# Sliding-window attention into an ELU layer pair on one core: two pairs taken together, casts and value copies moved to other engines, one batch's loads moved

## The chip, the cores and the metric

The kernel runs on one core of one Trainium2 chip. The metric is the device time of one execution in microseconds, lower is better. A core has a matmul engine (PE), a vector engine (DVE), an engine for activation functions (ACT), a general engine (POOL) and a synchronizing engine (SP). Each works through its own queue in order. SP, ACT and POOL also issue DMA transfers from their queues.

## The reference, cut to what matters

```python
# q, k, v: (8 batches, 8 heads, 576 positions, 64), float32
scores = (1 / sqrt(64)) * q @ k.transpose(0, 1, 3, 2)
scores = where(abs(pos[:, None] - pos[None, :]) <= 32, scores, -1e9)
attn = exp(scores - max(scores)); attn = attn / (sum(attn) + 1e-9)
x = (attn @ v) -> (4608 tokens, 512)          # heads side by side
h = x @ w_in                                  # w_in (512, 2048)
g = where(h > 0, h, exp(min(h, 0)) - 1)
out = g @ w_out                               # w_out (2048, 512), float32
```

## The kernel before, in words

Attention and the two dense layers run interleaved, in an order that is written out by hand (`tc.manual_schedule()`, L59): each engine's queue holds its instructions in the order in which the program emits them.

**The dense layers.** 4608 tokens make 18 tiles of 256. Of the 16 blocks of 128 hidden columns a step takes two, so a tile has 8 steps and the whole 144; the last loop (L639 ff.) counts them as `kk`. The first 16 steps alternate between tiles 0 and 1, from step 16 on tile t holds steps 8t to 8t+7. In step kk, `elu(kk-1)` emits one DVE instruction, g_sb (L607); then the tasks of slot "dve"; then `mm1(kk)` emits 8 matmuls 128x256 on PE (L583), the exponential e_sb on ACT (L590) and m_sb = e_sb - 1 on DVE (L596); then slot "mid"; then `mm2(kk-2)` emits 4 matmuls 128x512 (L622) and, at a tile's last step, one copy of y on ACT and one on DVE with their two output transfers on SP (L634, L635); then slot "end". `mm1` has two buffers, h0 and h1, in turn, so `mm1(kk+2)` needs g_sb of step kk to have been read out, and `mm2` needs g_sb as its weights.

**Attention.** Queries are taken in blocks of 64; a pair (`i`, 36 of them, two for each tile of the dense layers) is two blocks of all 8 heads. Against 128 keys per block: `scores` (32 products in pairs of heads, L297), `exponential` (ACT, 128x1024, L308), `mask` (DVE, L317), `pv` (L329, values with a column of ones), `normalize` (DVE, reciprocal and product, L338 and L341). The result x_st then goes to xT, the dense layers' operand, either by PE (`x_transpose`, L350, and `x_evac` on ACT) for pairs up to 9, or by a DMA transpose on SP (`x_dma`, L367) from pair 10 on. The scores, the products and the x transpose of a pair use one PSUM buffer of two banks, "s" or "u". `begin` (L509) gives each pair's first step. Pairs before 8 go one at a time, from `FIRST_TWO` on two together: scores in one step in "s" and "u", exponentials in that step and the next, masks one step later each, both products two steps after the scores, normalizing three and four steps after. Buffer "u" shares its banks with tile 1's y sums, and is theirs until step 18 (`swap_back`).

**What attention needs.** A batch has 4.5 pairs; batch 2 is first used by pair 9, batch 3 by pair 13, batch 4 by pair 18. Queries and keys are loaded as float32 by SP (`load_qk`, two transfers each, L123), cast to bf16 (`cast_qk`, on ACT or DVE by L227 and L229) and transposed. For batch 2 PE does that in four groups of nine with an evacuation by ACT (`transpose_qk`, L272, into qT and kT). From batch 3 on the cast rows are written to DRAM by a transfer from ACT's queue (`write_rows`, L253) and read back by a DMA transpose on SP (`transpose_rows`, L258). The casts of a batch from 3 on, six of them, go to the ends of the first free steps from `c0` on: steps in which no pair's scores or second exponential stand.

**Values.** `load_v` (POOL, L142, casting on the way) writes five blocks of 128 positions that start at -32: V_e, three buffers in turn. Odd query blocks need blocks shifted by 64, V_o: `rotate_v` (DVE, L153) copies halves of 64 partitions across, 64x1040 elements each, four instructions a batch. `hold_v` (L147) zeroes one row again on DVE: a load that follows has to wait for it.

Of the kernel before, what the change touches and what calls it, by code (L numbers as in the profile page):

```python
# [21 lines left out]
def kernel(  # L22
# [9 lines left out]
    nc = tc.nc  # L32
# [14 lines left out]
    VS = 5  # L47
# [46 lines left out]
    def ps_tile(shape, dt, tag, name):  # L94
# [7 lines left out]
          for i in range(2)]  # L102
    V_e = [cpool.tile([128, VS, H, VD], BF16, name=f"Ve{i}") for i in range(3)]
    V_o = [cpool.tile([128, VS - 1, H, VD], BF16, name=f"Vo{i}")
           for i in range(3)]
# [6 lines left out]
    WHOLE, HALF_A, HALF_B = (0, SJ), (0, SJ // 2), (1, SJ // 2)  # L112
# [37 lines left out]
    def rotate_v(b, m0, m1, parts=(0, 1)):  # L150
        e, o = V_e[b % 3], V_o[b % 3]
        for z in parts:
            nc.vector.tensor_copy(o[64 * z:64 * (z + 1), m0:m1],  # L153
                                  e[64 * (1 - z):64 * (2 - z),
                                    m0 + z:m1 + z])

# [30 lines left out]
    def edges(i):  # L189
# [19 lines left out]
        out=masks, in_=masks, compare_op=ALU.is_ge, fill=0.0,  # L209
        base=0, pattern=[[0, 5], [-1, QB]], channel_multiplier=1)  # L210
    nc.gpsimd.affine_select(
        out=masks, in_=masks, compare_op=ALU.is_ge, fill=0.0,
# [157 lines left out]
    def first_pair(b):  # L370
        return NQB * b // 2
# [27 lines left out]
    for mi in (0, 4):  # L399
        nc.gpsimd.affine_select(  # L400
            out=masks[:, mi, :], in_=masks[:, mi, :], compare_op=ALU.is_ge,
            fill=0.0, base=-WIN, pattern=[[0, QB]], channel_multiplier=1)
    nc.gpsimd.affine_select(
        out=masks[:, 3, :], in_=masks[:, 3, :], compare_op=ALU.is_ge,
# [16 lines left out]
    for i, tag in ((0, "s"), (1, "u")):  # L421
        scores(i, tag)
        exponential(i)
    idle(4, "y0")
    rotate_v(0, 0, 2)
    for i in (0, 1):
        mask(i)
# [34 lines left out]
    def at(kk, slot, fn, *args):  # L462
        tasks.setdefault((kk, slot), []).append((fn, args))
# [18 lines left out]
    for i in (2, 3):  # L482
        at(0, "mid", rotate_v, 0, 2, VS - 1, (i - 2,))
        at(0, "mid", mask, i)
        at(1, "mid", pv, i)
        at(2, "dve", normalize, i)
        at(3, "mid", x_transpose, i)
        at(3, "mid", x_evac, i, nc.scalar)
# [11 lines left out]
    for m in range(VS):  # L500
        at(16 + m, "mid", load_v, 2, m)
    at(12, "dve", rotate_v, 1, 0, 2)
    for z in range(2):
        at(14 + z, "dve", rotate_v, 1, 2, VS - 1, (z,))

    FIRST_TWO, FIRST_DMA, BACK_AT = 8, 10, 18
    begin = {4: 9, 5: 12, 6: 17, 7: 19, 8: 25, 10: 30, 12: 37}  # L509
    for i in range(FIRST_TWO, NPAIR):  # L510
        begin[i] = begin.get(i - i % 2, STEPS * (i // 2) - 14)
    for i in range(4, NPAIR):
        two = i >= FIRST_TWO
        kk, z = begin[i], i % 2 if two else 0
        at(kk, "end" if i == 4 else "mid", scores, i,
           "u" if z or i == 7 else "s")
        at(kk + z, "end" if i == 4 else "mid", exponential, i)
        at(kk + 1 + z, "dve", mask, i)
        at(kk + (2 if two else 1), "end", pv, i)
        n = kk + (3 + z if two else 2)  # L520
        at(n, "dve", normalize, i)
        if i < FIRST_DMA:
            at(n, "end", x_transpose, i)
            at(n, "end", x_evac, i, nc.scalar)
        else:
            at(n, "end", x_dma, i)
# [3 lines left out]
    for b in range(2, B):  # L530
        k0 = begin[first_pair(b)]

        l_qk, l_v, c0 = {2: (0, 0, 0), 3: (15, 24, 22)}.get(
            b, (k0 - 28, k0 - 22, k0 - 22))
        if b >= 3:
            at(l_qk, "mid", load_qk, b, 0, WHOLE)
            at(l_qk + 1, "mid", load_qk, b, 1, WHOLE)
            for m in range(VS):
                at(l_v + m, "mid", load_v, b, m)
        for n, back in enumerate((3, 2, 1, 0) if b == 2 else (10, 8, 3, 2)):  # L540
            m0 = 2 * (n // 2)
            at(k0 - back, "dve", rotate_v, b, m0, m0 + 2, (n % 2,))
        if b == 2:

            for n, (which, j0) in enumerate(((0, 0), (0, 9), (1, 0), (1, 9))):
                at(19 + n, "mid", cast_qk, b, which, WHOLE, j0, 9, nc.vector)
                at(20 + n, "mid", transpose_qk, b, which, WHOLE, j0, 9,
                   nc.scalar, "s")
            continue


        free = [f for f in range(c0, k0) if f not in starts]
        for n, (which, j0) in enumerate(
                (which, j0) for which in range(2) for j0 in (0, 6, 12)):
            at(free[n], "end", cast_qk, b, which, WHOLE, j0, 6,
               nc.vector if free[n] < 24 else nc.scalar)
            if j0 == 12:
                at(free[n], "end", write_rows, b, which)
                at(free[n] + (3 if free[n] == 29 else 4), "mid",
                   transpose_rows, b, which)  # L560
# [121 lines left out]
```

## Time and profile before

| what | us |
|---|---|
| median of 3 runs | 309.61 (308.73 to 309.79) |
| the profiled execution | 307.99 |
| its span, first to last instruction | 306.3 |
| PE busy | 295.2 |
| DVE busy | 245.5 |
| ACT busy | 169.1 |
| POOL busy | 47.9 |

The profile is one execution. Its times count from the span's first instruction. A timeline row gives start, length, engine, line, operation, what is written and read, how many were merged (x8), and in brackets idle time of the engine before it with what ended it. In the rows of a queue (SPq, ACTq) the length is that of issuing, waits within the issue included. "Start to start" is the distance between the starts of two neighbours on an engine: neighbouring instructions of ACT and DVE overlap by about 0.1 us, so their lengths can't be summed. The steps' places in the trace are told by the L583 groups: one opens at the start of each step (step 6 at 28.06, step 18 at 54.67, step 37 at 97.16).

### The profile page before, as it was taken

The page shows a single profiled execution, that of the slowest core. Times are in us where ns is not written, and L with a number is a line of the kernel's source. Part 1 is how long each engine was busy: PE and PEld are TensorE (multiplying, and loading weights), DVE is VectorE, ACT ScalarE, POOL GpSimd, SP SyncE. Part 2 cuts the span into 40 slices and gives each one's busy share as a digit, 9 for nine tenths or more (in the row PEclk, how much of TensorE's full clock was granted, in tenths as well). Part 3 has the DMA queues.
Part 4 walks back from the last instruction along what each step waited for, and adds up shares of the span by engine and source line. Part 5 has one row for each costly group of instructions (what it writes and reads, how often), then busy time and mean ns, then how long its engine had stood idle before and what let it go on. Part 6 is the DMA issues. An engine that isn't in the chain of part 4 may idle for free.

```text
span 306.3 us, 7611 instructions
## 1 busy us (share of the span) xinstructions
PE 295.2 (96%) x3083; PEld 196.6 (64%) x3083; DVE 245.5 (80%) x476; ACT 169.1 (55%) x254; POOL 47.9 (16%) x68
## 2 busy tenths in 40 slices
PE   7779999999999999999999999999999999999994
PEld 2466666676665666666666666666666666666662
DVE  6777688999978887988798879887988787877663
ACT  3663647677654674676367636763535353533431
POOL 8836002860220311111111100000000000000000
PEclk9999999999999999999999999999999999999999
DMA  9999999999999499999999897396111111111011
GB/s 188 186 205 205 183 295 411 280 148 176 270 250 190 40 253 257 294 220 218 161 321 195 226 227 276 111 196 144 68 36 71 34 71 35 71 36 68 0 70 68
DMA packets 91653, 51.74 MB, mean 169 GB/s; under 512 B 76515, under 2 KB 81635, under 8 KB 91619
## 3 DMA queue, kind: packets, MB, share of 16 engines
q0 software_dynamic: 42880, 10.10, 42.9%
q1 hardware_dynamic: 46866, 34.42, 41.8%
q10 hardware_dynamic: 1872, 6.75, 6.6%
q8 instruction: 24, 0.39, 0.6%
q14 instruction: 11, 0.08, 0.1%
HBM read 36.70 MB, written 15.34 MB: 170 GB/s over the span
## 4 chain that ended last, share of the span: by engine, by line
PE 84%; DVE 9%; ACT 2%; DMA 2%; issue 2%; ACTq 0%; DVEq 0%
PE ps L583 38%; PE psY L622 37%; PE psS L297 3%; PE psS L329 3%; DVE g_sb L607 2%; DMA f<-in_k_dram 2%; DVE pm L317 2%; DVE x_st L341 1%; DVE Vo L153 1%; DVE m_sb L596 1%; ACT pu L308 1%; PE psXT L350 1%; PE ptx L272 1%; ACT e_sb L590 1%; DVE y_sb L229 1%
## 5 line engine op out<-in xcount | busy, mean ns | idle before, releaser
L590 ACT ACTIVATE e_sb<-ps 128x512 f32<-128x512 f32 (+1 forms) x145 | 86.2, 595 | 121.8 <-PE ps L583 116.4
L583 PE MATMUL ps<-xT,w_in_sb 128*128 128x256 bf16 x1152 | 149.2, 273 | 1.0 <-DVE g_sb L607 0.6
L622 PE MATMUL psY<-w_out_sb,g_sb 128*128 128x512 bf16 x576 | 147.4, 379 | 0.0
L583 PEld LDWEIGHTS <-w_in_sb 128*128 128x128 bf16 x1152 | 110.8, 98 | 39.5 <-issue 1.6
L607 DVE SCALAR_TENSOR_TENSOR g_sb<-ps,m_sb 128x512 bf16<-128x512 f32 (+1 forms) x145 | 99.4, 686 | 12.5
L596 DVE TENSOR_SCALAR m_sb<-e_sb 128x512 bf16<-128x512 f32 x144 | 61.9, 430 | 35.6 <-ACT e_sb L590 33.6
L622 PEld LDWEIGHTS <-g_sb 128*128 128x128 bf16 x576 | 54.5, 98 | 38.6 <-DVE g_sb L607 0.2
L142 POOL DMA_DIRECT2D Ve<-in_v_dram x40 | 35.2, 888 | 123.4 <-PE psS L329 96.3
L308 ACT ACTIVATE pu<-psS 128x1024 bf16<-128x1024 f32 x36 | 36.5, 1019 | 1.6 <-PE psS L297 1.6
L341 DVE TENSOR_TENSOR x_st<-psS,rc 128x512 bf16<-128x512 f32 x36 | 24.9, 691 | 1.2
L317 DVE TENSOR_TENSOR pm<-pu,masks 128x1024 bf16<-128x1024 bf16 x36 | 24.6, 682 | 1.2 <-ACT pu L308 1.2
L227 ACT CAST qkb<-f 128x768 bf16<-128x768 f32 (+1 forms) x29 | 24.3, 838 | 0.0
L329 PEld LDWEIGHTS <-pm 128*64 128x64 bf16 x576 | 11.2, 110 | 11.3 <-DVE pm L317 8.2
L329 PE MATMUL psS<-Ve,pm 128*64 128x65 bf16 x320 | 13.9, 196 | 1.9 <-DVE pm L317 1.8
L153 DVE COPY Vo<-Ve 64x1040 bf16<-64x1040 bf16 x32 | 14.1, 442 | 1.2 <-DMA Ve<-in_v_dram 0.2
L229 DVE COPY y_sb<-psY 128x512 f32<-128x512 f32 x18 | 12.3, 685 | 1.0 <-PE psY L622 0.9
L329 PE MATMUL psS<-Vo,pm 128*64 128x65 bf16 x256 | 12.5, 197 | 0.5 <-DVE pm L317 0.2
L297 PEld LDWEIGHTS <-kT 64*128 64x128 bf16 x576 | 9.5, 95 | 5.1 <-issue 4.2
L297 PE MATMUL psS<-qT,kT 64*128 64x64 bf16 x576 | 11.9, 191 | 0.5 <-DVE kT L229 0.5
L227 ACT COPY y_sb<-psY 128x512 f32<-128x512 f32 x18 | 10.5, 582 | 2.2 <-PE psY L622 2.2
L227 ACT COPY qT<-ptx 128x1152 bf16<-128x1152 bf16 (+2 forms) x8 | 7.5, 971 | 3.2 <-PE ptx L272 2.4
L229 DVE CAST qkb<-f 128x1152 bf16<-128x1152 f32 (+3 forms) x11 | 7.7, 724 | 1.0 <-DMA f<-in_k_dram 0.6
(36 smaller groups left out, 70.9 us busy)
## 6 DMA issues: line engine op xcount, KB each, us to landing
out_dram<-y_sb SPq DMA_DIRECT2D x35, 256.0 KB, 2.5
f<-in_q_dram SPq DMA_DIRECT2D x12, 576.0 KB, 6.8
f<-in_k_dram SPq DMA_DIRECT2D x12, 576.0 KB, 7.4
in_dram<-qkb ACTq DMA_DIRECT2D x10, 576.0 KB, 4.8
Ve<-in_v_dram POOLq DMA_DIRECT2D x24, 128.0 KB, 7.2
w_in_sb<-in_moe_w_in_dram POOLq DMA_DIRECT2D x4, 512.0 KB, 9.9
w_out_sb<-in_moe_w_out_dram POOLq DMA_DIRECT2D x4, 512.0 KB, 12.8
Ve<-in_v_dram POOLq DMA_DIRECT2D x16, 96.0 KB, 7.4
```

The lines of the kernel that those rows point to most:

```text
L142: nc.gpsimd.dma_start(out=V_e[b % 3][p0:p1, m, :, 0:D], in_=v[b, :, lo + p0:lo + p1, :].rearrange("h p d -> p h d"))
L227: nc.scalar.copy(d_, s_)
L297: nc.tensor.matmul(psS[:, h % 2, hp * 128 + z * QB:hp * 128 + (z + 1) * QB], lhsT=kT[b % 2][base:base + 64, KPAD + hp * S + QB * qb - WIN: ...
L308: nc.scalar.activation(pu, _bap(psS, [psS.ap[0], [1, 1024]]), AX.Exp, scale=SCALE)
L317: nc.vector.tensor_mul(pm, pu, _bap(mm, [mm.ap[0], [0, H], [1, 2 * QB]]))
L329: nc.tensor.matmul(psS[QB * z:QB * (z + 1), par, hp * VD:(hp + 1) * VD], lhsT=pm[:, par * HP + hp, z * QB:(z + 1) * QB], rhs=vv[:, qb // 2 ...
L341: nc.vector.tensor_mul(x_st, _bap(psS, [psS.ap[0], [VD, HP], [512, 2], [1, D]]), _bap(rc, [rc.ap[0], [2, HP], [1, 2], [0, D]]))
L583: nc.tensor.matmul(ps[:, j, :], lhsT=w_in_sb[:, do, fo * 128:(fo + 1) * 128], rhs=xT[t][:, :, do, :], start=(do == 0), stop=(do == NDO - 1))
L590: nc.scalar.activation(e_sb, ps, AX.Exp)
L596: nc.vector.tensor_scalar(m_sb, e_sb, -1.0, None, ALU.add)
L607: nc.vector.scalar_tensor_tensor(g_t[kk][:, z * w:(z + 1) * w, :], ps, 0.0, m_t[kk][z], ALU.max, ALU.min)
L622: nc.tensor.matmul(psY[t][ts], lhsT=g_sb[:, j, ts * 128:(ts + 1) * 128], rhs=w_out_sb[:, s * FG + j, :], start=(s == 0 and j == 0), stop=( ...
```

## The change

Five things change; all lie between steps 15 and 58.

- Pairs 6 and 7 are taken together: `FIRST_TWO` is 6. Both scores go to step 18 (before 17 and 19), both products to step 20 (18 and 20), normalizing and x transposes to steps 21 and 22 (19 and 21). Pairs 8 and 9 begin at 26 in place of 25, pairs 10 and 11 at 31 in place of 30.
- Batch 2's casts stand at steps 18, 20, 21 and 23 (before 19 to 22), and the second and third are on ACT (all were on DVE). Its four groups of transposes stand at steps 22 to 25 (before 20 to 23), in "s" and "u" in turn (all in "s" before).
- The shifted copies of batches 2 and 3 are made by two SP transfers each, at steps 21 and 28, in place of eight DVE copies. Those of later batches stay on DVE.
- Batch 3's casts: free steps are now 22 to 25, 28, 29 (before 22, 23, 24, 27, 28, 29), and four of the six are on DVE (before two).
- Batch 4's loads of queries and keys stand at the end of step 35 (before the middle of steps 30 and 31, and so in SP's queue between batch 3's transposes of queries and of keys). Its values' loads keep their place in the program from step 36 on, but a `hold_v` at step 36 now holds them; before, POOL issued them as its queue got there, the first at 78.34 us, in step 28. Its casts begin at step 41 (before 36). The values' loads of batches 5 to 7 get a `hold_v` each too, and loads of queries and keys go to the ends of their steps in place of the middles.

In SP's queue the order becomes: queries of batch 3, tile 0's y, keys of batch 3, tile 1's y, shifted copies of batch 2, tile 2's y, shifted copies of batch 3, transposes of batch 3's queries and keys, tile 3's y, x transposes of pairs 10 and 11, queries and keys of batch 4.

```diff
+    def rotate_v_dma(b):
+        e, o = V_e[b % 3], V_o[b % 3]
+        for z in range(2):
+            nc.sync.dma_start(out=o[64 * z:64 * (z + 1), 0:VS - 1],
+                              in_=e[64 * (1 - z):64 * (2 - z), z:z + VS - 1])
...
-    FIRST_TWO, FIRST_DMA, BACK_AT = 8, 10, 18
-    begin = {4: 9, 5: 12, 6: 17, 7: 19, 8: 25, 10: 30, 12: 37}
+    FIRST_TWO, FIRST_DMA, BACK_AT = 6, 10, 18
+    begin = {4: 9, 5: 12, 6: 18, 8: 26, 10: 31, 12: 37}
...
-           "u" if z or i == 7 else "s")
+           "u" if z else "s")
...
-        l_qk, l_v, c0 = {2: (0, 0, 0), 3: (15, 24, 22)}.get(
+        l_qk, l_v, c0 = {2: (0, 0, 0), 3: (15, 24, 22), 4: (35, 36, 41)}.get(
             b, (k0 - 28, k0 - 22, k0 - 22))
         if b >= 3:
-            at(l_qk, "mid", load_qk, b, 0, WHOLE)
-            at(l_qk + 1, "mid", load_qk, b, 1, WHOLE)
+            at(l_qk, "end", load_qk, b, 0, WHOLE)
+            at(l_qk + (b != 4), "end", load_qk, b, 1, WHOLE)
+            if b > 3:
+                at(l_v, "dve", hold_v, b)
             for m in range(VS):
                 at(l_v + m, "mid", load_v, b, m)
-        for n, back in enumerate((3, 2, 1, 0) if b == 2 else (10, 8, 3, 2)):
-            m0 = 2 * (n // 2)
-            at(k0 - back, "dve", rotate_v, b, m0, m0 + 2, (n % 2,))
+        if b <= 3:
+            at((21, 28)[b - 2], "mid", rotate_v_dma, b)
+        else:
+            for n, back in enumerate((10, 8, 3, 2)):
+                m0 = 2 * (n // 2)
+                at(k0 - back, "dve", rotate_v, b, m0, m0 + 2, (n % 2,))
         if b == 2:
             for n, (which, j0) in enumerate(((0, 0), (0, 9), (1, 0), (1, 9))):
-                at(19 + n, "mid", cast_qk, b, which, WHOLE, j0, 9, nc.vector)
-                at(20 + n, "mid", transpose_qk, b, which, WHOLE, j0, 9,
-                   nc.scalar, "s")
+                at((18, 20, 21, 23)[n], ("mid", "end", "end", "mid")[n],
+                   cast_qk, b, which, WHOLE, j0, 9,
+                   (nc.vector, nc.scalar, nc.scalar, nc.vector)[n])
+                at(22 + n, "mid", transpose_qk, b, which, WHOLE, j0, 9,
+                   nc.scalar, "su"[n % 2])
             continue
...
             at(free[n], "end", cast_qk, b, which, WHOLE, j0, 6,
-               nc.vector if free[n] < 24 else nc.scalar)
+               nc.vector if free[n] < 26 else nc.scalar)
```

## The prediction

> **What bounds the kernel now.** I read, in this order: the page, PE's timeline (start of every first-layer group, L583, which opens a step), what PE waited for, then the timelines of ACT, DVE and SP around each late step, and the DMA table. Step n is iteration kk = n of the last loop.
>
> ```profile
> span 306.3 us, 7611 instructions
> PE 295.2 (96%) x3083; PEld 196.6 (64%) x3083; DVE 245.5 (80%) x476; ACT 169.1 (55%) x254; POOL 47.9 (16%) x68
> ```
> PE sets the end. But its busy time is modelled, so I take the distance between starts of the L583 groups instead.
>
> ```profile
> 74.02 1.04 PE L583 MATMUL ps<-xT,w_in_sb 128*128 128x256 bf16 x8
> ...
> 75.76 1.04 PE L583 MATMUL ps<-xT,w_in_sb 128*128 128x256 bf16 x8
> ...
> 80.44 0.40 PE L350 MATMUL psXT<-ident,x_st 128*128 128x128 bf16 x4 [0.26 <-DVE x_st L341]
> 80.68 1.04 PE L583 MATMUL ps<-xT,w_in_sb 128*128 128x256 bf16 x8
> ...
> 95.43 1.03 PE L583 MATMUL ps<-xT,w_in_sb 128*128 128x256 bf16 x8 [0.56 <-DVE g_sb L607]
> ```
> Step 26 (74.02 to 75.76) is a bare step: 1.74. What attention adds, from undisturbed steps: scores of one pair 0.44 (52.49 to 54.67), of two 0.68 (97.16 to 99.58); values' product of one pair 0.47 (43.41 to 45.63), of two 0.73 (101.32 to 103.79); nine transposes 0.50; an x transpose 0.23. From step 38 (99.58) on every step has its sum. The starts of steps 17 to 37:
> ```
> 17 52.49  18 54.67  19 57.20  20 59.62  21 62.34  22 64.81  23 67.05
> 24 69.63  25 71.61  26 74.02  27 75.76  28 78.27  29 80.68  30 82.64
> 31 85.06  32 86.80  33 89.49  34 91.24  35 92.97  36 95.43  37 97.16
> ```
> Length less sum of contents (step 28, say: 2.40 - 1.74 - 0.23 = 0.43): late are step 18 by 0.32, 23 by 0.34, 24 by 0.24, 27 by 0.05, 28 by 0.43, 32 by 0.22, 35 by 0.72, together 2.32 us; PE waits for DVE each time the profile names one. That is all the change can win beside PE work itself. Steps 14 and 15 lose 0.4 more, untouched.
>
> ```profile
> 93.70 0.42 DVE L153 COPY Vo<-Ve 64x1040 bf16<-64x1040 bf16 x1
> 94.16 0.43 DVE L596 TENSOR_SCALAR m_sb<-e_sb 128x512 bf16<-128x512 f32 x1
> 94.69 0.69 DVE L607 SCALAR_TENSOR_TENSOR g_sb<-ps,m_sb 128x512 bf16<-128x512 f32 x1
> ```
> The late g_sb of step 35 stands behind a shifted copy of batch 3's values. One limit stands close behind:
>
> ```profile
> 77.96 1.22 SPq L123 DMA_DIRECT2D f<-in_q_dram  x2
> 79.22 2.19 SPq L123 DMA_DIRECT2D f<-in_k_dram  x2
> 90.56 5.02 SPq L258 DMA_TRANSPOSE kT<-in_dram  x1
> ```
> ```profile
> kT<-in_dram SPq DMA_TRANSPOSE x5, 7.8
> ```
> The first three are SP's issues (start, length), the last the median from issue to landing. Batch 3's keys land at 90.56 + 7.8 = 98.4; step 37 reads them at 98.13 + 0.34 = 98.47. Any gain ahead of step 37 would be lost to this landing if it stayed put. (Landings of single transfers below are the trace's semaphore records.)
>
> **The Trainium skill.** "SBUF — State Buffer", section "Who interferes with whom": copies and casts of DVE in two-port modes and a GpSimd instruction exclude each other. The trace agrees in kind: L153 takes 424 ns at least and 871 beside POOL's issues. "DMA: Bandwidth & Descriptors", section "Issuing engines are not separate DMA queues": transfers of all queues share 16 engines and interleave. The trace fits: batch 3's keys took 6.3 us into DRAM (84.19 to 90.54) beside batch 4's loads, 3.6 (72.05 to 75.62) without.
>
> **Part by part.**
> ```profile
> 63.42 0.60 ACT L590 ACTIVATE e_sb<-ps 128x512 f32<-128x512 f32 x1 [0.94 <-PE ps L583]
> 63.92 1.28 ACT L227 COPY qT<-ptx 128x1152 bf16<-128x1152 bf16 x1
> 65.09 0.58 ACT L227 COPY xT<-psXT 128x512 bf16<-128x512 bf16 x1
> ```
> ACT's prices are taken start to start like these, where it is never idle: e_sb 0.50, evacuation of nine transposes 1.17, x evacuation 0.49, cast 128x1152 1.04 (47.21 to 48.25), cast 128x768 0.73, y 0.49, own DMA issue 0.7. DVE: g 0.60, m 0.53, mask 0.60, reciprocal and x_st about 0.9, y 0.60, shifted copy 0.45.
>
> *Pairs 6 and 7 together.* Scores go from steps 17 and 19 to 18, products from 18 and 20 to 20. PE saves 2 x 0.44 - 0.68 = 0.20 and 2 x 0.47 - 0.73 = 0.21. Step 18's stall goes: mask 6 now has two steps. Next late: pair 7's scores need the two banks of tile 1's y; DVE's y copy ends about 1.15 after step 18 starts, the scores come at 1.30: free by 0.15, and a shortfall costs itself.
>
> *Casts and transposes of batch 2, one or two steps later.* Two 128x1152 casts leave DVE (2 x 0.67) for ACT (2 x 1.04); batch 3 gives DVE two 128x768 casts more (2 x 0.47) and takes them from ACT (2 x 0.73). DVE's late steps 23 and 24 (0.34 + 0.24) should go: the two casts that ran 1.96 together at 67.02 become one of 1152 and one of 768, and the shifted copies of steps 22 to 25 are gone. But ACT becomes late in step 22. I follow its queue from pair 6's x transpose: start of that evacuation 0.42 after it, evacuation 0.49, cast of keys 1.04, e_sb(22) 0.50, evacuation of queries 1.17, pair 7's x evacuation 0.59 to its end, 0.05 of signal: 4.26. The transposes of step 23 take that bank ("u"). PE arrives there after the rest of step 21 (0.22), step 22 (1.74 + 0.50 + 0.23 = 2.47) and its own first layer (0.97): 3.66. A new stall of 0.60; bounds 0.4 (the shortest evacuation of nine, 1.01, 51.83 to 52.84) and 1.0 (DMA issue or casts slow, as one DVE cast of 1122 ns was). It gives later steps slack: e_sb(25), behind step 24's DMA issue, is late by 0.4, absorbed since mm1 of step 27 asks for g(25) only 0.4 after it is done; batch 2's second key evacuation ends 0.3 before pair 9's scores.
>
> *Shifted copies by DMA.* DVE loses 8 x 0.45 = 3.6 us at steps 22 to 25, 27, 29, 34 and 35. With DVE's prices, from step 33's start: exponential 11 ends at 0.86, g(32) at 1.10, mask 11 at 1.78 (its product due at 2.18), y at 2.65, g(33) at 3.25, normalizing 10 at 4.2, m(34) at 4.7, g(34) at 5.4 (mm1 of step 36 due at 5.95), normalizing 11 at 6.2, m(35) at 6.8, g(35) at 7.5 (mm1 of 37 due at 7.69). The same count from step 28 has mask 9 at 1.8 (due 2.2), x_st 8 at 3.8 (due 4.3), x_st 9 at 6.2 (due 6.3). So the 0.05 + 0.43 + 0.22 + 0.72 go. Each batch is two SP transfers of 64 x 2080 bf16, 266 KB; nearest row: y's 256 KB, landing 2.5 us after issue (bounds 2.5 and the 7.2 of values' loads under load). Batch 2's values land by 65.4, perhaps 68 as a load of keys of batch 3 now runs beside them; copies land by 75 at worst, used near 79. SP waits for that landing; behind it stand only tile 2's y (due near 74) and batch 3's pair, then its transposes. These need the values' landing at 74.7 and have until 95. Cost 0; uncovered, pair 9 would wait one for one.
>
> *Batch 4's loads to steps 35 and 36, its casts to 41, 44 to 48.* SP reaches batch 3's key transpose without loads ahead: cast in step 29 ends near 83, lands in DRAM near 87, transposed near 92 to 95; due now at 96.5. The limit above goes. Next due: queries of batch 4. SP issues them behind pair 11's x transpose, second half near 95.7; ACT reads at the end of step 41, near 104.8: 9 us, against 6.8 median for this load. Batch 4's key transposes: written near 118.8, before took 14.6 from write to landing (116.33 to 130.93), so 133.4, due 136.5. Both cost 0 if these hold. Four zeroings of 62 ns on DVE in bare or light steps: 0.
>
> Sum: 0.41 + 2.32 = 2.73 won, 0.60 lost: 2.1 us. The profiled execution took 307.99 (1.7 around its span) and would take 305.9. The median shown, 309.61, is 1.6 above that execution; the same 2.1 off it gives 307.5.
>
> **Rivals.**
> A, forecast: one stall at step 23. 307.5.
> B, no stall at step 23. For: the short evacuation takes 0.16 off, and an x evacuation that starts early would take more. Against: every link of the 4.26 is a measured one. 309.61 - 2.73 = 306.9.
> C, new stalls at several places beside step 23: my counts leave margins of 0.1 to 0.4 at pair 7's scores, pair 9's scores, x_st 9 and g(35), and DVE copies and casts beside POOL's issues ran 0.4 over. Against: each stall of PE gives the others that time back. Three of them missed by 0.4: 1.2 more, 307.5 + 1.2 = 308.7.
> D, slower: queries of batch 4 land late at step 41, and ACT's cast holds e_sb(42) and all behind it. They share engines with keys and five values' loads released at step 36, which before were spread over 78 to 107. Bounds: 5.6 us as for batch 5's first half, and 12.5 (45.63 to 58.09, behind eleven other loads). Beyond 9.1 + 0.6 of slack each us is lost; the 2.1 is gone at 11.8, a landing after 13 gives 3.3 - 2.1 = 1.2 slower, 310.8.
> That the new order isn't built is excluded: the built queues stand as described.
>
> **How the numbers follow.** A 0.48, B 0.12, C 0.25, D 0.15. About 0.3% (0.93 us) can be told from no change. Faster: A, B and a third of C, 0.68; same 0.17; slower 0.15. The range leaves out D and a little at the low end: 306.3 (B, with 0.6 of spread as the runs had) to 309.8.
>
> **What would show it.** Right: pairs 6 and 7 as x32 groups; steps 18, 24, 27, 28, 32, 35 at their sums; in step 23 PE's transposes held by an ACT evacuation for about 0.6; SP's key transpose of batch 3 landing before 95. Wrong: steps 24 to 27 longer than 2.24, 2.24, 2.42, 1.74 (C); ACT's cast at step 41 waiting for a query load (D); steps 32 to 35 still late, which would say the shifted copies were not their cause.

## The result, and the profile after

The changed kernel is slower: 319.58 us (median of 4 runs, 317.20 to 320.19) against 309.37 for the kernel before, a ratio of 1.0317 [1.0261, 1.0373]. The forecast was 307.5. Here and below medians are over all runs, while ratios leave out runs more than 1.5% above the fastest of their kernel, and a kernel of which only one run would then be left has no ratio.

The page of the changed kernel's profiled execution (319.71 us) begins so; the row "PE" below is its busy share in 40 slices of 7.9 us.

```profile
span 317.9 us, 7623 instructions
PE 298.8 (94%) x3083; PEld 199.3 (63%) x3083; DVE 241.5 (76%) x472; ACT 169.5 (53%) x254; POOL 48.8 (15%) x68
...
PE   8789999999999999943999999999999999999994
```
PE has the same 3083 matmuls and is no longer at 96%: one hole of two slices near 140 us holds the loss. What PE waited for (total, times, longest):

```profile
PE psS L304 <- DMA kT<-in_dram: 9.4, 1, 9.4
```
The scores (L304) waited once, for 9.4 us, for keys read back from DRAM. PE's timeline tells which scores: the row with the bracket.

```profile
137.48 1.04 PE L597 MATMUL ps<-xT,w_in_sb 128*128 128x256 bf16 x8
147.92 1.03 PE L304 MATMUL psS<-qT,kT 64*128 64x64 bf16 x32 [9.40 <-DMA kT<-in_dram]
...
150.57 1.70 PE L597 MATMUL ps<-xT,w_in_sb 128*128 128x256 bf16 x7
```
The first row opens step 58, which has the first use of batch 4 (pairs 18 and 19). The first-layer groups at L597 after the change are those of L583 before; their distances, added up, account for the difference of the two profiled executions:

| steps | before | after | difference |
|---|---|---|---|
| 2 and 3 | 4.25 | 5.58 | +1.3 |
| 17 to 57 | 85.42 | 83.68 | -1.7 |
| 58 | 2.42 | 13.09 | +10.7 |
| 59 | 1.74 | 3.40 | +1.7 |

The sum is 11.9, beside 11.7 between the two executions. The first row is no part of the change: from 20.8 to 24.2 PE's granted clock was 0.50 in this execution and 1.00 in that of the kernel before, and executions of the kernels below have the short or the long form, with either schedule. Without it 10.6 remain, beside 10.2 between the medians.

**Where the keys of batch 4 were.** SP's queue after the change (SPq: start and length of the issue). L123 loads batch 5's queries and keys, L265 transposes batch 4's; L260 on ACT's queue writes the rows of batch 4's keys to DRAM.

```profile
118.56 1.23 SPq L123 DMA_DIRECT2D f<-in_q_dram  x2
119.83 1.25 SPq L123 DMA_DIRECT2D f<-in_k_dram  x2
121.19 10.28 SPq L265 DMA_TRANSPOSE qT<-in_dram  x1
...
132.68 8.00 SPq L265 DMA_TRANSPOSE kT<-in_dram  x1
```
```profile
121.11 0.55 ACTq L260 DMA_DIRECT2D in_dram<-qkb  x1
```
The same transfers in the kernel before (there L258 transposes, L253 writes):

```profile
111.57 2.24 SPq L258 DMA_TRANSPOSE qT<-in_dram  x1
...
117.27 1.66 SPq L123 DMA_DIRECT2D f<-in_q_dram  x2
...
120.37 1.25 SPq L123 DMA_DIRECT2D f<-in_k_dram  x2
121.72 5.93 SPq L258 DMA_TRANSPOSE kT<-in_dram  x1
```
```profile
116.33 0.55 ACTq L253 DMA_DIRECT2D in_dram<-qkb  x1
```
After the change again, POOL's queue at the same time; the bracket is POOL's idle time before.

```profile
128.81 4.46 POOL L142 DMA_DIRECT2D Ve<-in_v_dram  x5 [27.53 <-PE psS L336]
```
Batch 5's four loads move 2.4 MB from 118.6 on; the last lands at 131.47. Batch 4's keys, sent to DRAM by ACT at 121.11 into the same traffic, arrive there at 131.64 (10.5 us; in the kernel before, sent at 116.33, 5.2). The transpose of the queries is held in SP's queue until 131.46, within 0.01 us of the last load's landing. The transpose of the keys, issued at 132.68, therefore had to wait for two things: its rows (131.64) and its queue, in which the queries' transpose and two transfers of y were issued until 132.56. With the queue free it could have started 1.0 us earlier and no more, because the rows were not there. By then batch 5's values, five loads that were released together at 128.81, are under way beside it. The keys land at 147.87; PE was ready for them at 138.52.

In the kernel before, the queries' transpose and the write of the keys' rows stand ahead of batch 5's loads, and only the keys' transpose behind them. The casts of batch 4 now stand five steps later (41 for 36), and batch 5's loads, at steps 46 and 47, did not move. Nobody changed a line of batch 5's keys and queries but for the slot; the order of the transfers changed all the same.

The chain of waits of the same stretch (start, length, what):

```profile
132.68 15.19 DMA kT<-in_dram
147.87 0.05 issue
```
15.19 from issue to landing, where the median of this tile's transposes is 5.3. Had one read the chain alone, the transfer would look slow; the queues show that it also started 11 us late.

**After the wait.** The rows of the windows view give the stretch, its length, PE's busy time, PEld, DVE, ACT, POOL, then the granted clock of PE, and at the end GB/s.

```profile
138.00:148.00 10.00, 0.60 (x9) 0.30 (x9) 2.19 (x4) 1.22 (x2) 0.00 (x0) 0.78 1.26 210
148.00:152.00 4.00, 4.00 (x43) 2.44 (x44) 0.69 (x1) 1.02 (x1) 0.00 (x0) 0.50 1.15 285
```
PE idles for 9.4 us, and comes back at half the clock. That is the 3.40 of step 59, and it makes 1.7 of the loss there and 1.3 in step 58 (10.7 more than before, of which 9.4 are the wait).

### The profile page after: what moved, and what is told of

Read it like the earlier page. It is cut to its first block, busy times and chain, and to the rows that moved or that the text cites. A ratio compares the mean times of both kernels' runs of the same rounds, so it can differ in the third digit from the quotient of the medians.

```text
span 317.9 us, 7623 instructions
## 1 busy us (share of the span) xinstructions
PE 298.8 (94%) x3083; PEld 199.3 (63%) x3083; DVE 241.5 (76%) x472; ACT 169.5 (53%) x254; POOL 48.8 (15%) x68
## 4 chain that ended last, share of the span: by engine, by line
PE 85%; DMA 7%; POOL 2%; ACT 2%; DVE 2%; issue 1%; POOLq 0%; DVEq 0%; ACTq 0%
PE ps L597 38%; PE psY L636 38%; DMA kT<-in_dram 5%; PE psS L336 3%; PE psS L304 3%; DMA w_in_sb<-in_moe_w_in_dram 2%; PE ptx L279 1%; POOL Ve L142 1%; POOL c L136 1%; PE psXT L357 1%; DVE pm L324 1%; ACT pu L315 1%; ACT qkb L234 1%; DVE g_sb L621 0%; PE ptx L274 0%
## 5 line engine op out<-in xcount | busy, mean ns | idle before, releaser
L597 PE MATMUL ps<-xT,w_in_sb 128*128 128x256 bf16 x1152 | 151.3, 275 | 0.7 <-DMA w_in_sb<-in_moe_w_in_dram 0.6
L636 PE MATMUL psY<-w_out_sb,g_sb 128*128 128x512 bf16 x576 | 149.1, 383 | 0.0
L597 PEld LDWEIGHTS <-w_in_sb 128*128 128x128 bf16 x1152 | 111.8, 99 | 40.5 <-issue 1.1
L142 POOL DMA_DIRECT2D Ve<-in_v_dram x40 | 35.5, 900 | 153.9 <-PE psS L336 92.2
L304 PE MATMUL psS<-qT,kT 64*128 64x64 bf16 x576 | 12.2, 193 | 9.9 <-DMA kT<-in_dram 9.4
L304 PEld LDWEIGHTS <-kT 64*128 64x128 bf16 x576 | 9.9, 97 | 14.4 <-DMA kT<-in_dram 9.7
L336 PEld LDWEIGHTS <-pm 128*64 128x64 bf16 x576 | 11.1, 110 | 10.5 <-DVE pm L324 7.9
L236 DVE COPY y_sb<-psY 128x512 f32<-128x512 f32 x18 | 12.3, 685 | 1.2 <-PE psY L636 1.1
L234 ACT COPY y_sb<-psY 128x512 f32<-128x512 f32 x18 | 10.5, 583 | 2.2 <-PE psY L636 2.2
L153 DVE COPY Vo<-Ve 64x1040 bf16<-64x1040 bf16 x24 | 10.4, 431 | 0.8
L395 PE MATMUL ps_idle<-zeros 128*128 128x512 bf16 x19 | 7.3, 525 | 1.3 <-DVE zeros L194 1.3
```

Of the source, the lines that this page charges most:

```text
L142: nc.gpsimd.dma_start(out=V_e[b % 3][p0:p1, m, :, 0:D], in_=v[b, :, lo + p0:lo + p1, :].rearrange("h p d -> p h d"))
L234: nc.scalar.copy(d_, s_)
L304: nc.tensor.matmul(psS[:, h % 2, hp * 128 + z * QB:hp * 128 + (z + 1) * QB], lhsT=kT[b % 2][base:base + 64, KPAD + hp * S + QB * qb - WIN: ...
L336: nc.tensor.matmul(psS[QB * z:QB * (z + 1), par, hp * VD:(hp + 1) * VD], lhsT=pm[:, par * HP + hp, z * QB:(z + 1) * QB], rhs=vv[:, qb // 2 ...
L597: nc.tensor.matmul(ps[:, j, :], lhsT=w_in_sb[:, do, fo * 128:(fo + 1) * 128], rhs=xT[t][:, :, do, :], start=(do == 0), stop=(do == NDO - 1))
L636: nc.tensor.matmul(psY[t][ts], lhsT=g_sb[:, j, ts * 128:(ts + 1) * 128], rhs=w_out_sb[:, s * FG + j, :], start=(s == 0 and j == 0), stop=( ...
```

## The experiments

Two theories stood at the start. *Late casts*: the transposes of batch 4 got behind batch 5's loads in SP's queue. (That the write of the rows got among the same loads was not asked; no run below tests it apart.) *Bunched values*: `hold_v` packs the values of batch 5, which before had trickled in, into the moment at which batch 4's keys are transposed. A third question was whether the rest of the change brought what the forecast said. All edits are to the changed kernel unless said otherwise; ratios are against the kernel before on the same chip (its median there 308.9 to 309.2).

**Batch 4's part undone.** Loads of batch 4 where they were, casts from 36.

```diff
-        l_qk, l_v, c0 = {2: (0, 0, 0), 3: (15, 24, 22), 4: (35, 36, 41)}.get(
+        l_qk, l_v, c0 = {2: (0, 0, 0), 3: (15, 24, 22)}.get(
...
+            sl = "mid" if b == 4 else "end"
-            if b > 3:
+            if b > 4:
                 at(l_v, "dve", hold_v, b)
```


> The changed kernel with batch 4's part alone undone: its loads at steps 30 and 31, its casts from step 36, no hold of its values' loads. Theory (batch 4's key transpose lands 10 us late because its casts moved 3 to 5 steps later, behind batch 5's loads in SP's queue): step 58 takes 2.4 us again and the 12.3 us of steps 58 and 59 are gone. Rival (pairs, casts or shifted copies cause it): step 58 stays above 10 us. My forecast's side claim, that batch 3's keys then become the limit: step 37 stalls by 1 to 4 us, since batch 4's loads stand ahead of that transpose again and the shifted copies too. Sum: 1.7 us below before without that stall, up to 2.3 us above it with 4.

Measured: 311.27 (20 runs), 1.0047 [1.0022, 1.0072]. Step 58 is 2.42, without a wait. But what PE waited for now reads

```profile
PE psS L304 <- DMA kT<-in_dram: 2.5, 1, 2.5
PE psS L336 <- DMA Vo<-Ve: 0.9, 1, 0.9
```
and the first stands at step 37, for batch 3's keys.

```profile
100.41 0.40 PE L304 MATMUL psS<-qT,kT 64*128 64x64 bf16 x8 [2.47 <-DMA kT<-in_dram]
```
So the damage of 10 belongs to batch 4's part, and something has to be done with batch 4's loads all the same: left between batch 3's transposes, they make batch 3's keys the limit, as the prediction said of step 37 (step 37 takes 5.98, and 38 2.21 in place of 1.74). The second row is a shifted copy of values that comes late, beside three loads of values that POOL now issues from 68.87 on; in the changed kernel it issues none between 62 and 97.

**Batch 5's values held longer.**

```diff
-        ... 4: (35, 36, 41)}.get(
+        ... 4: (35, 36, 41), 5: (46, 57, 52)}.get(
```


> The changed kernel with the values' loads of batch 5 held five steps longer (57 in place of 52). If batch 5's loads of queries and keys ahead in SP's queue are the whole cause, the key transpose of batch 4 is issued as late as before (132.7) and step 58 still stalls by 8 us or more. If the five values' loads that take the DMA engines from 132 to 138 us are a needed part, tile 5's y and the key transpose go through directly after 132, the keys land near 138 to 140, and step 58 stalls by 0 to 2 us: 308 to 311 us in all.

Measured: 311.17 (20 runs), 1.0036 [1.0010, 1.0063]. SP's queue:

```profile
120.02 9.17 SPq L265 DMA_TRANSPOSE qT<-in_dram  x1
130.41 2.39 SPq L265 DMA_TRANSPOSE kT<-in_dram  x1
```
The transpose of the queries stands behind batch 5's loads as in the changed kernel (9.17), and the keys' rows reach DRAM as late (129.40). The transpose of the keys, without the values beside it, is issued in 2.39 and lands at 137.37 in place of 147.87; step 58 takes 2.54. On this kernel the values' loads at that place therefore make most of the 9.4. The price turned up elsewhere: they land up to 154, their shifted copies on DVE are late, and steps 64 to 72 lose about 5.6 us, PE waiting for g_sb behind them (3.6 us in one wait).

**Batch 4's part alone, on the kernel before**, with `hold_v` for batch 4 and for no later one.

```diff
+        ... 3: (15, 24, 22), 4: (35, 36, 41)}.get(
...
+            sl = "end" if b == 4 else "mid"
+            if b == 4:
+                at(l_v, "dve", hold_v, b)
```


> The kernel before with batch 4's part of the change alone: loads at step 35, values held to step 36, casts from step 41. Theory: this part alone does the damage, step 58 stalls by 9 to 10.5 us and step 59 loses 1.7 more at the lower clock: about 320 to 321 us. Rival (the part needs the others, such as the shifted copies in SP's queue): within 2 us of before.

Measured: 310.38 (9 runs), 1.0055 [1.0031, 1.0080]: a miss, 1 us where 9 to 10.5 had been expected. PE waits 0.9 us for these keys. POOL's queue differs: the values of batch 5 are spread, and only two of their loads stand in the critical stretch.

```profile
98.54 7.01 POOL L142 DMA_DIRECT2D Ve<-in_v_dram  x8 [32.37 <-DVE m_sb L599]
...
131.15 1.65 POOL L142 DMA_DIRECT2D Ve<-in_v_dram  x2 [14.63 <-PE psS L329]
```

**The same with the holds of batches 5 to 7**, and loads at the ends of steps: batch 4's part complete, on the kernel before.

```diff
+            at(l_qk, "end", load_qk, b, 0, WHOLE)
+            at(l_qk + (b != 4), "end", load_qk, b, 1, WHOLE)
+            if b > 3:
+                at(l_v, "dve", hold_v, b)
```


> The kernel before with batch 4's part and also the holds of the values' loads of batches 5 to 7 and the loads' places at the ends of their steps: all that the change does from step 30 on, without pairs, casts and shifted copies. If the holds' bunch of five loads at step 52 turns the 0.9 us of the run without them into the 10 us of the changed kernel, step 58 stalls by 6 us or more, about 318 us. If not (rival: the earlier parts of the change are needed for the damage), by 0 to 2 us, 309 to 311 us.

Measured: 319.78 (4 runs), 1.0372 [1.0301, 1.0443]. By the median the damage is whole again. In the profiled execution (316.88, the shortest of its runs) step 58 takes 8.60 and step 59 3.21; the queues look like those of the changed kernel:

```profile
122.56 9.06 SPq L258 DMA_TRANSPOSE qT<-in_dram  x1
132.81 5.57 SPq L258 DMA_TRANSPOSE kT<-in_dram  x1
```
and batch 5's five values' loads are issued together at 130.19. So batch 4's part as it was made, with the holds, gives the loss by itself; none of the other four parts is needed for it, and on this kernel the holds of the later batches, with the slot of the loads, turn 1 us into 10.

**The changed kernel without the holds of batches 5 to 7.**

```diff
-            if b > 3:
+            if b == 4:
                 at(l_v, "dve", hold_v, b)
```


> The changed kernel without the new holds of the values' loads of batches 5 to 7 (batch 4's stays). Theory now: the 10 us at step 58 need two things at once, batch 4's late casts that put its two transposes behind batch 5's loads, and the five values' loads of batch 5 bunched at step 52 by their hold, between the two transposes. Then here, with those loads spread from about 101 us on as POOL's queue comes to them, the keys of batch 4 land 0 to 2 us late: step 58 stalls by 0 to 2 us, 307.5 to 310 us in all. Rival (the late casts are enough, the run with batch 4's part alone was lucky): step 58 stalls by 6 us or more.

Measured: 318.85, 309.56, 320.19 and 315.83; the runs are too far apart for a ratio or a verdict. The expectation, that the loss would go with the bunch, was missed in three of the four runs. In the profiled one (318.85) the values of batch 5 are spread, two loads in the critical stretch, and yet

```profile
124.73 9.33 SPq L265 DMA_TRANSPOSE qT<-in_dram  x1
...
135.29 8.06 SPq L265 DMA_TRANSPOSE kT<-in_dram  x1
```
with a wait of 7.7 us at step 58. One run is without the loss, and has no trace. What holds in the traces of both kernels is that the transposes and the write of the rows are behind batch 5's loads; why that costs 1 us in one and 10 in the other is not shown.

**Batch 5's loads behind batch 4's transposes** (loads, and the values' hold, at 52, casts from 58).

```diff
+        ... 4: (35, 36, 41), 5: (52, 52, 58)}.get(
```


> The changed kernel with batch 5's loads of queries and keys at step 52, behind batch 4's key transpose in SP's queue, its values' loads held to step 52 as in the changed kernel, its casts from step 58. Theory (batch 5's loads ahead of the transposes are a needed part): batch 4's queries are transposed by 124, its keys by 131, no stall at step 58. Rival (the bunched values' loads alone delay the transposes): step 58 stalls by 3 us or more. Batch 5's own transposes may then be late at step 74; only step 58 is read.

Measured: 320.04 (one run). Step 58 takes 2.42, and SP's queue shows the two transposes as they are with no load ahead:

```profile
119.26 2.36 SPq L265 DMA_TRANSPOSE qT<-in_dram  x1
125.20 2.61 SPq L265 DMA_TRANSPOSE kT<-in_dram  x1
```
The keys land at 130.25, and batch 5's loads follow at 127.87. But batch 5's casts, late in their turn, meet batch 6's loads: PE waits 9.9 us for batch 5's keys at step 74. The same fault, one batch on, at the same price, in this one run: it is not tied to batch 4.

**Batch 4's loads right behind batch 3's transposes**, at the end of step 32, and casts from 36 as in the kernel before.

```diff
-        ... 4: (35, 36, 41)}.get(
+        ... 4: (32, 36, 36)}.get(
```


> The changed kernel with batch 4's loads at the end of step 32, directly behind batch 3's key transpose, and its casts from step 36 as before. Theory: batch 3's keys are in time as in the changed kernel (they landed at 91.5, due at 98), batch 4's key rows are written at step 45 again and its transposes are done by 132, due at 138: no stall at 37 or 58, and the 1.7 us that steps 17 to 57 won stay: about 307.6 us, ratio 0.994. Rival (transposes are late for another reason): a stall of several us at 37 or 58.

Measured: 306.86 (6 runs), 0.9924 [0.9903, 0.9945]. Batch 3's keys land at 90.85, the limit at step 37 is gone, and the transposes are where they were:

```profile
110.08 2.54 SPq L265 DMA_TRANSPOSE qT<-in_dram  x1
...
119.29 1.25 SPq L123 DMA_DIRECT2D f<-in_k_dram  x2
120.63 6.78 SPq L265 DMA_TRANSPOSE kT<-in_dram  x1
```
Queries ahead of batch 5's loads, keys behind them, and the rows of the keys in DRAM at 118.61, as those loads began. Step 58 has its 2.42, although batch 5's values are bunched here too, from 128.28. All that differs from the changed kernel is the place of batch 4's loads and casts: 12.7 us between the medians.

**Only the casts two steps earlier** (39 for 41), loads where the change put them.

```diff
-        ... 4: (35, 36, 41)}.get(
+        ... 4: (35, 36, 39)}.get(
```


> The changed kernel with batch 4's casts from step 39 instead of 41 (39, 40, 41, 44, 45, 46), all else the same: the query transpose then stands at step 45, ahead of batch 5's loads in SP's queue, the key transpose at 50, still behind them. Theory (it takes both transposes behind those loads): the keys land near 131, no stall at step 58, about 307 to 308 us. Rival (one transpose behind them, with the bunched values' loads, is enough): step 58 stalls by 3 us or more.

Measured: 306.46 (20 runs), 0.9928 [0.9907, 0.9949].

```profile
113.48 2.25 SPq L265 DMA_TRANSPOSE qT<-in_dram  x1
...
120.28 1.25 SPq L123 DMA_DIRECT2D f<-in_k_dram  x2
122.77 8.54 SPq L265 DMA_TRANSPOSE kT<-in_dram  x1
```
The queries' transpose is back ahead of the loads, the keys' alone is behind; the keys' rows, sent at 116.67, reach DRAM at 120.36, before any of the loads has landed. The time was a little better than expected. The landing was not: 137.99, where I had expected 131; the issue lasts until 131.31, and by then the values (from 127.84) are under way. Step 58 takes 2.98, so the keys come about 0.6 too late even here.

Two more runs ask about the other parts, with batch 4 as in the version that put its loads at step 32.

**The first key cast of batch 2 on ACT one step later.**

```diff
-                at((18, 20, 21, 23)[n], ("mid", "end", "end", "mid")[n],
+                at((18, 20, 22, 23)[n], ("mid", "end", "end", "mid")[n],
```


> The version with batch 4's loads at step 32, and the first cast of batch 2's keys at the end of step 22 instead of 21 on ACT, behind pair 7's x evacuation. My forecast's account of step 23 (that cast makes ACT late, 0.7 us of stall): step 23 takes 2.3 us instead of 2.9, 306.2 us in all. Rival (another cause): step 23 unchanged, 306.9 us.

Measured: 306.62 (11 runs), 0.9940 [0.9912, 0.9968]. Step 23 takes 2.28, so the stall is gone and that cast was its cause. But the total can't be told from 0.9924: 0.14 us came back at step 24 and 0.34 at step 39. Most of the larger one is a wait for the DMA transpose of x for tile 5, which stands behind batch 4's loads in SP's queue: it landed at 103.23 (102.35 without this edit), and step 40's first layer waited 0.25 us for it.

**The shifted copies of batches 2 and 3 on DVE again.**

```diff
-        if b <= 3:
-            at((21, 28)[b - 2], "mid", rotate_v_dma, b)
...
+        for n, back in enumerate((3, 2, 1, 0) if b == 2 else (10, 8, 3, 2)):
```


> The version with batch 4's loads at step 32, and the shifted copies of batches 2 and 3 on DVE again, at 3, 2, 1, 0 and 10, 8, 3, 2 steps ahead as before. If those copies were what made steps 27, 28 and 32 to 35 late, about 0.4 to 1.2 us come back there: 307.3 to 308.1 us. Rival (the later start of pairs 8 to 11 did it): those steps stay at their sums, 306.9 us.

Measured: 308.71 (14 runs), 0.9993 [0.9972, 1.0014]. Against the version with the copies by DMA steps 28, 30, 35 and 36 are longer by 0.38, 0.30, 0.08 and 0.81: 1.6 us of the 1.85 between the medians. The DMA copies are worth about that, more than the 0.4 to 1.2 expected. Steps 27 and 32, late in the kernel before, stay at their sums.

## Why the prediction was wrong

**The step that failed** reads: "Batch 4's key transposes: written near 118.8, before took 14.6 from write to landing (116.33 to 130.93), so 133.4, due 136.5. Both cost 0 if these hold." They were written at 121.11, 2.3 later than this says, but were due 2.0 later too (138.52). What failed is the 14.6: they took 26.8, landing at 147.87. The term that was 14.6 consists of the rows' way into DRAM, the time until the transpose is issued, and the transpose: 5.2 + 0.2 + 9.2 before, 10.5 + 1.0 + 15.2 after. I moved the casts of batch 4 and carried over a duration that was measured in another order of transfers. In the new order the casts' delay takes the write of the rows and both transposes past batch 5's four loads; I had counted what those transposes needed from the casts, and not what they were moved past. Those loads stand in the timeline that I had read, at 117.27 to 121.62 in the kernel before, between the two transposes; and the dearer write beside loads (6.3 us for batch 3's keys, 3.6 for its queries without batch 4's loads) is in the prediction itself. The runs with casts at 36 (and the loads at 32), 39 and 41 (306.86, 306.46, 319.58) show the step's true form: with the rows written ahead of the loads and the keys' transpose alone behind them it costs nothing, or 0.6; with the write and both transposes behind them, and the values bunched, 9.4.

**The second half of the same step**, "Four zeroings of 62 ns on DVE in bare or light steps: 0", priced `hold_v` as DVE's time. Its effect is on POOL: it releases five loads at once, at 128.81, in the stretch where the keys are transposed. Held longer they take most of the stall away; without them batch 4's part costs 1 us on the kernel before, and with them 10. On the changed kernel taking the holds away was not enough. So the cause that every profiled run with the loss at step 58 shares is that batch 4's casts came too late to be ahead of batch 5's loads, and the bunch is what makes it long; how the two share the 9.4 was not settled. Nor was it tested whether the held queue or the late rows matter more. The landings speak for the rows: in the five kernels with casts at 41 and the loads ahead of both transposes the rows reached DRAM between 129.40 and 132.15, and the keys' transpose was issued 1.0 to 1.6 us later, in the one without the holds 4.6.

**Rival D had the right batch and the wrong place.** It had the slower side from batch 4's queries arriving late at ACT's cast in step 41. That cast starts at 107.14, right behind ACT's y copy (106.68, 0.46 start to start), without a gap. D did not happen. I looked for the risk where the moved loads are read, and not at what the moved casts set off.

**What held.** Pairs 6 and 7, and the late steps: steps 18, 20, 24, 27, 28, 32 and 35 are at the sums of their contents (2.43, 2.48, 2.24, 1.74, 2.48, 1.74 and 1.74), and batch 3's keys landed at 91.52, before the 95 that was named. The new stall at step 23 was sized at 0.60 and is 0.68 (2.92 against 2.24), and it stands where it was put, PE's transposes behind the evacuation on ACT:

```profile
68.18 0.66 PE L279 MATMUL ptx<-ident,qkb 128*128 128x128 bf16 x9 [0.52 <-ACT xT L234]
```
ACT's queue ahead of it, the cast of keys first to be late:

```profile
64.36 0.58 ACT L234 COPY xT<-psXT 128x512 bf16<-128x512 bf16 x1 [0.49 <-PE psXT L357]
64.84 1.16 ACT L234 CAST qkb<-f 128x1152 bf16<-128x1152 f32 x1
65.90 0.60 ACT L604 ACTIVATE e_sb<-ps 128x512 f32<-128x512 f32 x1
66.38 1.29 ACT L234 COPY qT<-ptx 128x1152 bf16<-128x1152 bf16 x1
67.54 0.59 ACT L234 COPY xT<-psXT 128x512 bf16<-128x512 bf16 x1
```
From 64.36 to 68.13 is 3.77 in five pieces, each within 0.02 of its price. Two of the dangers that rival C named came true: step 30 missed by 0.13 (x_st of pair 9, margin 0.1), and step 39 by 0.11 (DVE beside POOL's issues, below). So 1.74 were won of the 2.1 forecast: 0.08, 0.13 and 0.11 make the difference but for 0.04. The version with only batch 4's place changed gains 1.76 over the same steps, and 2.35 by its ratio (0.9924 of 309.0; 1.7 to 3.0 by the interval): the sum for the rest of the change was right within that, and one term priced at 0 was 12.3, the excess of steps 58 and 59.

**What is open.** Why late casts without bunched values cost 1 us on the kernel before and up to 10 on the changed one: both have the transposes behind the same loads, and their runs vary by 6 and 11 us. And what part the late rows have, which would take a run that writes the rows early and leaves both transposes behind the loads.

## What to carry to other kernels

When an instruction that issues or feeds a transfer is moved, write down the order of the issuing queue before and after, and ask of each moved transfer, and of the one that feeds it from another queue, which loads now stand ahead of it or run beside it; a landing time measured in the old order is no price in the new one. A hold that costs an engine 62 ns may also bunch transfers that had been spread; place the burst against the due times of other transfers. And where a queue repeats batch by batch, delay of one batch meets the next batch's loads, so a mended place has to be looked at one period later as well.

## What the runs showed of the hardware

- *The DMA transpose of a batch's queries or keys can hold its queue until the loads ahead have landed.* Issue of the transpose ended, and the last load ahead landed, at 131.46 and 131.47 (changed kernel), 127.65 and 127.64 (before), 127.41 and 127.46 (loads at 32), 129.19 and 129.19 (values held). With no loads ahead the issue took 2.36 and 2.61. Why is not shown, and the small transposes of x were not held so: with the loads at 32 one was issued from 129.83 to 131.06, while a transfer of y ahead of it landed at 133.23. The Trainium skill, "DMA: Bandwidth & Descriptors", section "Queues, rings and completion order", has it that each DMA engine takes descriptors in the order of a queue's ring and goes round between queues; the trace agrees in that the keys' transpose landed after the SP loads ahead of it, while values from POOL's queue, issued later than those loads, landed before it. It does not say that the issue itself is held.
- *An idle PE comes back slow.* In the wait of 9.4 us the granted clock fell to 0.50 at 143.7, and it stayed there until 153.9; the next step took 3.40 for 1.74. In the wait of 2.5 us (batch 4's part undone) it fell at 100.0 and stayed at 0.50 until 103.4; the next step took 2.21. "TensorE: Matmul & The Clock Gate", section "HAM oscillation — how this bites in real kernels", warns of gaps above about 3.4 us; here 2.5 did it too, so a stall of PE can cost more than its length. What decides is not shown: waits of 0.6 and 0.9 us at step 58 had no such effect, but steps 2 and 3 of the changed kernel ran at 0.50 after waits of at most 0.8 us, much like those of the kernel before.
- *DVE beside a burst of POOL's loads.* One m_sb (at 100.75) took 0.78 beside five issues of batch 4's values (97.01 to 101.28), the next 0.42: the 0.11 of step 39. This agrees with "SBUF — State Buffer", section "Who interferes with whom", as in the prediction, in kind.
- *A shifted copy by DMA* (64x2080 bf16, 266 KB) took 3.4 to 6.3 us from issue to landing on the changed kernel, within the 2.5 to 7.2 that the prediction had taken; beside loads of values that were not held back (batch 4's part undone) up to 10.4, and there PE waited for it.
